# Attention with a gated second branch: PE mode runs over two row blocks, wider query-weight and key loads

## The chip, the cores and the metric

The kernel runs on one core of a Trainium2 chip. The metric is the device time of one launch in microseconds (us), the median over several runs. A profiled execution has a span a little shorter than its device time (933.1 us of 934.86 us before); both are used, and it is said which. The engines are named as in the profile: PE is the matmul engine, PEld its weight loads, DVE the vector engine, ACT the scalar engine, POOL is GpSimd, SP the queue from which most transposing transfers are issued.

## The reference

A layer norm, an attention with 32 heads of width 192 over the last 512 cached keys, and a gated feed-forward branch that multiplies the attention's output.

```python
# x: 1 x 2048 x 640; k_cache, v_cache: 1 x 32 x 2048 x 192; wq: 640 x 6144; wo: 6144 x 640
xn = _layernorm(x)
q = (xn @ wq) as 32 heads of 192
k, v = k_cache[:, :, -512:], v_cache[:, :, -512:]
p = softmax(q k^T * 192**-0.5)
s = (p v) merged over heads @ wo
g = silu((sigmoid(xn @ w_gate) * (xn @ w_up)) @ w_down)
return x + s * g
```

## The kernel before

The feed-forward branch comes first (about 165 us). The attention then goes over 16 pairs of heads in 8 groups of two pairs (`G = 2`, `NG = 8`), and for each group over 4 row blocks of 512 queries (`NST = 4`): 32 blocks. A head has 192 = 3 x 64 elements (`PC = 3`), so the query and score matmuls contract over 64 rows. Two of them run at once, one in rows 0 to 63 of the array and one in rows 64 to 127 (`LO`, `HI`). The value and output matmuls contract over all 128 rows. I call these the two modes of PE.

```python
def stage_q(n, u):                       # 20 matmuls, 64 rows: queries of the next block
    ...
    for c in range(NCD):
        for h in range(2):
            for b, r in enumerate((LO, HI)):
                nc.tensor.matmul(ps[:, b, :], lhsT=wq_t[g][r, u, 2 * c + h]..., rhs=x[s][r, c, :], ...)
    nc.vector.tensor_copy(qT_t[n][:, 2 * u:2 * u + 2, :], ps)

def stage_s(n, pp, c):                   # 6 matmuls, 64 rows: scores, then exp on ACT
    ...
def stage_pv(n, pp, i):                  # 16 matmuls, 128 rows: values of one head
    if i == 0:
        ost_t[0] = ost_pool.tile([P, TQ, 2 * DH], BF16, name="o_st")     # ost_pool: bufs=2
    ...                                  # DVE: reciprocal, then o_st = ps * reciprocal
    if i == 1:
        oT = oT_pool.tile([P, TQ * PC, P], BF16, name="oT")
        nc.sync.dma_start_transpose(oT[:], o_st[:]...)                   # read by stage_wo
def stage_wo(n, q):                      # 12 matmuls, 128 rows: output projection
    ...
for n, (g, s) in enumerate(blocks):      # 32 blocks
    for k, (pp, c) in enumerate(todo):   # 8 score stages, 3 query stages: 64 rows
        stage_s(n, pp, c)
        if k % 2 == 1 and k // 2 < G * PC // 2 and n < last:
            stage_q(n + 1, k // 2)
    ...                                  # loads ahead
    for k, u in enumerate(pv):           # 4 value stages, 4 output stages of block n - 1: 128 rows
        stage_pv(*u)
        if wo:
            stage_wo(*wo[k])
```

PSUM, the memory that the matmuls write to, is used as a ring of four slots of two banks (`bank2`). A stage takes the next slot and has to wait until the stage four before it has been read out. `o_st` takes the finished values of a pair of heads for one block, and a DMA transposes it into `oT`.

The softmax here doesn't subtract the row's maximum and nothing guards it: scores larger than these inputs give would overflow.

Of the kernel before, what the change touches and what calls it, by code (L numbers as in the profile page):

```python
# [9 lines left out]
ALU = mybir.AluOpType  # L10
BF16 = mybir.dt.bfloat16
# [4 lines left out]
def kernel(  # L16
# [72 lines left out]

    rs = dict(side="right")  # L90
    xnt_pool = ctx.enter_context(tc.tile_pool(name="xnt_pool", bufs=1, **rs))
    wq_pool = ctx.enter_context(tc.tile_pool(name="wq_pool", bufs=2, **rs))
    k_pool = ctx.enter_context(tc.tile_pool(name="k_pool", bufs=2, **rs))
    kt_pool = ctx.enter_context(tc.tile_pool(name="kt_pool", bufs=2 * G, **rs))
    v_pool = ctx.enter_context(tc.tile_pool(name="v_pool", bufs=1, **rs))

    HF = 64
# [3 lines left out]
    xnS = [xnt_pool.tile([P, NCD, 512], BF16, name=f"xnS{s}") for s in range(NST)]  # L101
    xnT = [xnt_pool.tile([P, NCD, 512], BF16, name=f"xnT{s}") for s in range(NST)]

    NV = 4 * G
    v_tiles = []
    for i in range(NV):
        vt = v_pool.tile([P, KC, DH + 2], BF16, name=f"v_sb{i}")
# [7 lines left out]

    k_of = {}

    def load_k(hp, eng):

        k_sb = k_pool.tile([P, KC * PC, 2, HF], BF16, name="k_sb")  # L120
        for i in range(2):
            hk = (2 * hp + i) // rep
            eng.dma_start(
                k_sb[:, :, i, :],
                A_k_cache[0, hk, Sk - W:Sk, :].rearrange("(p k) (j e) -> p (k j) e", k=KC, j=PC),
            )
        k_of[hp] = k_sb

    def load_v(hp, eng):
        v_t[hp] = []  # L130
        for i in range(2):
            hk = (2 * hp + i) // rep
            vt = v_tiles[(2 * hp + i) % NV]
            eng.dma_start(
                vt[:, :, 0:DH],
                A_v_cache[0, hk, Sk - W:Sk, :].rearrange("(p j) d -> p j d", j=KC),
            )
            v_t[hp].append(vt)

    def load_wq(hp, eng):  # L140


        if hp % G == 0:
            wq_t[hp // G] = wq_pool.tile([P, G * PC // 2, NCD * 2, 2, HF], BF16, name="wqp")
        wqp = wq_t[hp // G]
        for j in range(PC):
            jj = (hp % G) * PC + j
            r = HI if jj % 2 else LO
            for i in range(2):
                d0 = (2 * hp + i) * DH + j * HF  # L150
                eng.dma_start(
                    wqp[r, jj // 2, :, i, :],
                    wq_r[:, :, :, d0:d0 + HF].rearrange("p c h n -> p (c h) n"),
                )

    def turn_k(hp):
        kT = kt_pool.tile([P, KC * PC, P], BF16, name="kT")
        nc.sync.dma_start_transpose(kT[:], k_of[hp][:].rearrange("p k i e -> p (k i e)"))
        kT_t[hp] = kT


    with ExitStack() as bctx:
# [147 lines left out]
        for s in range(NST):  # L310
# [40 lines left out]
            nc.sync.dma_start(xnS[s][HI], xnT[s][LO])  # L351
            if s == 0:
                for hp in range(G):
                    load_k(hp, nc.gpsimd)
                for hp in range(G):
                    load_v(hp, nc.gpsimd)
                    load_wq(hp, nc.gpsimd)
            elif s == 1:
                for hp in range(G):
                    turn_k(hp)  # L360


    acc_pool = ctx.enter_context(tc.tile_pool(name="acc_pool", bufs=1))
    wo_pool = ctx.enter_context(tc.tile_pool(name="wo_pool", bufs=2))
    qT_pool = ctx.enter_context(tc.tile_pool(name="qT_pool", bufs=2))
    e_pool = ctx.enter_context(tc.tile_pool(name="e_pool", bufs=2))
    ost_pool = ctx.enter_context(tc.tile_pool(name="ost_pool", bufs=2))
    oT_pool = ctx.enter_context(tc.tile_pool(name="oT_pool", bufs=2 * G))
    small = ctx.enter_context(tc.tile_pool(name="small", bufs=8))
    fin = ctx.enter_context(tc.tile_pool(name="fin", bufs=2))  # L370
    fout = ctx.enter_context(tc.tile_pool(name="fout", bufs=4))
    gate_pool = ctx.enter_context(tc.tile_pool(name="gate_pool", bufs=TQ + 2))

    acc = [acc_pool.tile([P, D], F32, name=f"acc{t}") for t in range(NST * TQ)]
    wo_t = {}

    def load_wo(g, eng):
        wo_g = wo_pool.tile([P, G * PC, D], BF16, name="wo_g")
        eng.dma_start(wo_g[:], wo_r[:, g * G * PC:(g + 1) * G * PC, :])
        wo_t[g] = wo_g  # L380

    def load_ahead(g, s):


        if s < G:
            load_wq(g * G + s, nc.scalar)
            load_k(g * G + s, nc.scalar)
        elif s == G:
            for hp in range(g * G, (g + 1) * G):
                load_v(hp, nc.scalar)  # L390
                turn_k(hp)
        if s == NST - 1:
            load_wo(g, nc.scalar)



# [1 line left out]

    def stage_q(n, u):

        g, s = blocks[n]
        if u == 0:
            qT_t[n] = qT_pool.tile([P, G * PC, 512], BF16, name="qT")
        ps = bank2()
        for c in range(NCD):
            for h in range(2):
                for b, r in enumerate((LO, HI)):
                    x = xnT if b == h else xnS
                    nc.tensor.matmul(  # L409
                        ps[:, b, :], lhsT=wq_t[g][r, u, 2 * c + h].rearrange("p i e -> p (i e)"),  # L410
                        rhs=x[s][r, c, :],
                        start=(c == 0 and h == 0), stop=(c == NCD - 1 and h == 1),
                    )
        nc.vector.tensor_copy(qT_t[n][:, 2 * u:2 * u + 2, :], ps)  # L414

    def stage_s(n, pp, c):

        g, s = blocks[n]
        kT, qT = kT_t[g * G + pp], qT_t[n]
        if c == 0:  # L420
            E_t[n, pp] = e_pool.tile([P, KC, 2, 512], BF16, name="E")
        ps = bank2()
        for j in range(PC):
            for b, r in enumerate((LO, HI)):
                nc.tensor.matmul(  # L425
                    ps[:, b, :], lhsT=kT[r, c * PC + j, :], rhs=qT[r, pp * PC + j, :],
                    start=(j == 0), stop=(j == PC - 1),
                )
        nc.scalar.activation(E_t[n, pp][:, c, :, :], ps, AF.Exp, scale=scale_qk)  # L429
# [60 lines left out]
                )  # L490

    def finish(ps, gB_sb, t, d0, d1):
        t_sb = fin.tile([P, D], F32, name="t_sb")
        o_sb = fout.tile([P, D], BF16, name="o_sb")
        d = slice(d0, d1)
        nc.vector.tensor_tensor(t_sb[:, d], ps, gB_sb[:, d], ALU.mult)  # L496
        nc.vector.tensor_tensor(o_sb[:, d], t_sb[:, d], acc[t][:, d], ALU.add)  # L497
        nc.sync.dma_start(of[t * P:(t + 1) * P, d], o_sb[:, d])

    gates = {}  # L500
# [1 line left out]
    def stage_wo(n, q):  # L502
        g, s = blocks[n]
        t = s * TQ + q
        gB_sb = gates.get(t)
        if n == last and q == TQ - 1:

            ps, h = bank2(), D // 2
            for i in range(2):
                wo_mm(ps[:, i, :], n, q, [(i * h, h)], i * h)  # L510
                finish(ps[:, i, 0:h], gB_sb, t, i * h, (i + 1) * h)
            return
        oA = flat(bank2())
        wo_mm(oA, n, q, d_chunks)
        if g == NG - 1:
            finish(oA[:, 0:D], gB_sb, t, 0, D)
        elif g == 0:
            nc.vector.tensor_copy(acc[t][:], oA[:, 0:D])
        else:
            nc.vector.tensor_tensor(acc[t][:], oA[:, 0:D], acc[t][:], ALU.add)  # L520
        if g == NG - 2:
            prep_last(t)

    blocks = [(g, s) for g in range(NG) for s in range(NST)]
    last = len(blocks) - 1
    qT_t, E_t, oT_t, ost_t = {}, {}, {}, {}
    load_wo(0, nc.gpsimd)
    for u in range(G * PC // 2):
        stage_q(0, u)
    for n, (g, s) in enumerate(blocks):  # L530

        todo = [(pp, c) for pp in range(G) for c in range(KC)]
        for k, (pp, c) in enumerate(todo):
            stage_s(n, pp, c)
            if k % 2 == 1 and k // 2 < G * PC // 2 and n < last:
                stage_q(n + 1, k // 2)
        if g + 1 < NG:
            load_ahead(g + 1, s)
        for m in (n - 1, n) if n == last else (n - 1,):
            if n > 0 and blocks[m][0] == NG - 1:  # L540
                for t in range(blocks[m][1] * TQ, blocks[m][1] * TQ + TQ):
                    gates[t] = load_gate(t, nc.scalar)

        pv = [(n, pp, i) for pp in range(G) for i in range(2)]
        wo = [(n - 1, q) for q in range(TQ)] if n > 0 else []
        if n < last:
            for k, u in enumerate(pv):
                stage_pv(*u)
                if wo:
                    stage_wo(*wo[k])  # L550
        else:
            for k, u in enumerate(pv):
                stage_pv(*u)
                if k == 1:
                    stage_wo(*wo.pop(0))
            for u in wo:
                stage_wo(*u)
    for q in range(TQ):
        stage_wo(last, q)

# [28 lines left out]
```

## Time and profile before

| | before |
|---|---|
| device time | 934.81 us, later 934.77 us (4 runs, 934.43 to 934.86) |
| span of the profiled execution | 933.1 us |
| PE busy, matmuls | 924.7 us, 8025 |
| first query matmul to the end | 768.35 us of the span |
| one block: 64-row part, 128-row part | 11.76 us, 12.07 us |
| changes between the two modes in the attention | 63 |

First the page of the profile: the busy times of the engines, the clock granted to PE in 40 equal slices (tenths of full speed, 9 is 90% or more), and the DMA packets.

```profile
PE 924.7 (99%) x8025; PEld 539.4 (58%) x8025; DVE 451.2 (48%) x643; ACT 303.8 (33%) x340; POOL 87.9 (9%) x107
...
PEclk9999999999999999999999999999999999999999
...
DMA packets 271681, 87.18 MB, mean 93 GB/s; under 512 B 250289, under 2 KB 268785, under 8 KB 271601
```

PE is busy throughout at full clock. That alone does not say that it works at its peak, since matmuls overlap in the record. The starts tell more. In time order, a matmul with 512 columns is followed after 215 to 216 ns, one with 193 columns after 86 ns, one with 128 columns after 56 ns. The two matmuls of a 64-row pair start 2 to 4 ns apart, the next pair 213 ns later.

One group line of the page, the loading of query weights into the array (line, engine, operation, shapes and count, busy us, mean ns of one, idle time before it):

```profile
L409 PEld LDWEIGHTS <-wqp 64*128 64x128 bf16 x1920 | 93.4, 94 | 113.8 <-issue 0.3
```

The timeline of PE through one whole block shows the two modes (start us, duration us, engine, line, operation, output<-inputs, shapes, count):

```profile
402.98 1.47 PE L425 MATMUL ps_all<-qT,kT 64*128 64x512 bf16 x12
...
413.35 1.46 PE L425 MATMUL ps_all<-qT,kT 64*128 64x512 bf16 x12
414.74 1.54 PE L441 MATMUL ps_all<-v_sb_97,E 128*128 128x193 bf16 x16
416.11 1.79 PE L486 MATMUL ps_all<-wo_g,oT 128*128 128x512 bf16 x12
...
426.81 1.47 PE L425 MATMUL ps_all<-qT,kT 64*128 64x512 bf16 x12
```

The 64-row part takes 414.74 - 402.98 = 11.76 us, the 128-row part 426.81 - 414.74 = 12.07 us. At the border the pace breaks: from the last score matmul to the first value matmul it is 308 ns start to start instead of 213, and from the last output matmul to the next score matmul 152 ns instead of 56. After the change the second and third value matmuls follow at 94 and 88 ns before the pace of 86 is reached, and after the change back the second score pair follows at 223 ns instead of 213. Where the stage changes but not the mode, the pace holds: 85 to 86 ns from a value to an output matmul, 55 to 56 from an output to a value matmul, 212 to 213 between query and score pairs. So the break goes with the change of mode and not with the change of stage. Such a change of mode comes 63 times.

### The profile page before, as it was taken

Reading aid. Unit: us, or ns where it says so; the run is one execution under the profiler, and the core shown is the slowest. Engines: PE = TensorE matmul, PEld = TensorE weight load, DVE = VectorE, ACT = ScalarE, POOL = GpSimd, SP = SyncE. Lnnn points to the kernel's source line nnn. Section 1 sums busy time; section 2 is a strip of 40 time slices with the busy share of each in tenths; the row PEclk is TensorE's granted clock in tenths of the full one; section 3 lists DMA queues with packets and bytes.
Section 4 is the critical chain, followed back from the end, with each engine's and each line's share of the span. In section 5 each row is a group of like instructions: output and inputs, shape, how many; then the busy total and the mean of one; then the engine's idle time right before and its main releaser. Section 6 shows DMA issues by size and latency. Waiting matters only on the chain. (4 is left out here: it accounts for less than half of the span.)

```text
span 933.1 us, 18277 instructions
## 1 busy us (share of the span) xinstructions
PE 924.7 (99%) x8025; PEld 539.4 (58%) x8025; DVE 451.2 (48%) x643; ACT 303.8 (33%) x340; POOL 87.9 (9%) x107
## 2 busy tenths in 40 slices
PE   8999999999999999999999999999999999999997
PEld 5545445565555555555555555555665665665665
DVE  4443532454444444444444444444444444444657
ACT  4333322433333333333333333333333333333340
POOL 0070000100000000000000000000000006665000
PEclk9999999999999999999999999999999999999999
DMA  9566030376334533463346324633563348553435
GB/s 286 151 125 119 15 98 15 96 111 102 82 58 70 107 77 55 73 121 77 47 71 113 63 70 70 106 68 77 73 106 70 77 73 152 125 130 77 91 91 148
DMA packets 271681, 87.18 MB, mean 93 GB/s; under 512 B 250289, under 2 KB 268785, under 8 KB 271601
## 3 DMA queue, kind: packets, MB, share of 16 engines
q1 hardware_dynamic: 146864, 47.20, 25.9%
q10 hardware_dynamic: 121136, 27.40, 14.9%
q0 software_dynamic: 3600, 11.41, 4.8%
q8 instruction: 63, 1.03, 0.5%
q14 instruction: 18, 0.14, 0.1%
HBM read 44.70 MB, written 5.24 MB: 54 GB/s over the span
## 5 line engine op out<-in xcount | busy, mean ns | idle before, releaser
L429 ACT ACTIVATE E<-ps_all 128x1024 bf16<-128x1024 f32 x256 | 247.8, 1022 | 496.2 <-PE ps_all L425 443.8
L486 PE MATMUL ps_all<-wo_g,oT 128*128 128x512 bf16 (+2 forms) x1536 | 228.2, 299 | 0.0
L414 DVE CAST qT<-ps_all 128x1024 bf16<-128x1024 f32 x96 | 117.6, 1225 | 226.3 <-PE ps_all L409 226.3
L425 PE MATMUL ps_all<-qT,kT 64*128 64x512 bf16 x1536 | 186.7, 376 | 0.0
L441 PEld LDWEIGHTS <-E 128*128 128x128 bf16 x2048 | 171.0, 98 | 24.4 <-issue 13.6
L486 PEld LDWEIGHTS <-oT 128*128 128x128 bf16 x1536 | 121.4, 97 | 76.2
L409 PEld LDWEIGHTS <-wqp 64*128 64x128 bf16 x1920 | 93.4, 94 | 113.8 <-issue 0.3
L425 PEld LDWEIGHTS <-kT 64*128 64x128 bf16 x1536 | 72.3, 94 | 91.8 <-issue 8.4
L448 DVE TENSOR_TENSOR o_st<-ps_all,rden 128x768 bf16<-128x768 f32 x128 | 122.6, 958 | 4.8 <-DVE rden L447 0.5
L447 DVE RECIPROCAL rden<-ps_all 128x4 f32<-128x4 f32 x128 | 23.3, 182 | 98.2 <-PE ps_all L441 98.1
L477 POOL TENSOR_TENSOR acc_1573<-acc_1573,gBa_sb 128x640 f32<-128x640 f32 x1 | 1.4, 1399 | 603.4 <-DVE acc_1573 L520 603.4
L325 DVE TENSOR_TENSOR hT_sb<-ps_all,sig_sb 128x512 bf16<-128x512 f32 x48 | 33.1, 692 | 51.0 <-PE ps_all L319 41.1
L409 PE MATMUL ps_all<-xnT_94,wqp 64*128 64x512 bf16 x240 | 55.7, 376 | 0.0
L409 PE MATMUL ps_all<-xnT_96,wqp 64*128 64x512 bf16 x240 | 55.7, 376 | 0.0
L409 PE MATMUL ps_all<-xnT_95,wqp 64*128 64x512 bf16 x240 | 55.7, 376 | 0.0
L409 PE MATMUL ps_all<-xnS_90,wqp 64*128 64x512 bf16 x240 | 55.6, 376 | 0.0
L409 PE MATMUL ps_all<-xnS_92,wqp 64*128 64x512 bf16 x240 | 55.6, 376 | 0.0
L409 PE MATMUL ps_all<-xnS_91,wqp 64*128 64x512 bf16 x240 | 55.6, 376 | 0.0
L409 PE MATMUL ps_all<-xnT_93,wqp 64*128 64x512 bf16 x240 | 55.4, 376 | 0.0
L409 PE MATMUL ps_all<-xnS_89,wqp 64*128 64x512 bf16 x240 | 55.3, 376 | 0.0
L339 PE MATMUL ps_all<-wd_sb,hT_sb 128*128 128x512 bf16 (+1 forms) x384 | 52.8, 299 | 0.0
L324 ACT ACTIVATE sig_sb<-ps_all 128x512 bf16<-128x512 f32 x48 | 28.6, 597 | 56.6 <-PE ps_all L319 56.2
(159 smaller groups left out, 681.6 us busy)
## 6 DMA issues: line engine op xcount, KB each, us to landing
wqp<-in_A_wq_dram ACTq DMA_DIRECT2D x84, 80.0 KB, 3.0
wo_g<-in_A_wo_dram ACTq DMA_DIRECT2D x7, 960.0 KB, 5.3
k_sb<-in_A_k_cache_dram ACTq DMA_DIRECT2D x28, 192.0 KB, 4.8
gB_d<-gB_sb POOLq DMA_DIRECT2D x16, 160.0 KB, 2.4
gBa_sb<-gB_d POOLq DMA_DIRECT2D x16, 160.0 KB, 3.6
xa_sb<-in_A_x_dram POOLq DMA_DIRECT2D x16, 160.0 KB, 3.5
gBa_sb<-gB_d ACTq DMA_DIRECT2D x16, 160.0 KB, 3.0
out_dram<-o_sb SPq DMA_DIRECT2D x15, 160.0 KB, 1.8
```

Of the source, the lines that this page charges most:

```text
L324: nc.scalar.activation(sig_sb[:], gu[:, 0, :], AF.Sigmoid)
L325: nc.vector.tensor_tensor(hT_sb[:, f, :], gu[:, 1, :], sig_sb[:], ALU.mult)
L339: nc.tensor.matmul(oB_ps[:, d0:d0 + dsz], lhsT=hT_sb[:, f, q * P:(q + 1) * P], rhs=wd_sb[:, f, d0:d0 + dsz], start=(f == 0), stop=(f == NF ...
L409: nc.tensor.matmul(ps[:, b, :], lhsT=wq_t[g][r, u, 2 * c + h].rearrange("p i e -> p (i e)"), rhs=x[s][r, c, :], start=(c == 0 and h == 0), ...
L414: nc.vector.tensor_copy(qT_t[n][:, 2 * u:2 * u + 2, :], ps)
L425: nc.tensor.matmul(ps[:, b, :], lhsT=kT[r, c * PC + j, :], rhs=qT[r, pp * PC + j, :], start=(j == 0), stop=(j == PC - 1),)
L429: nc.scalar.activation(E_t[n, pp][:, c, :, :], ps, AF.Exp, scale=scale_qk)
L441: nc.tensor.matmul(o_ps[:, q // 2, q % 2, 0:DH + 1], lhsT=E[:, c, i, q * P:(q + 1) * P], rhs=vt[:, c, 0:DH + 1], start=(c == 0), stop=(c = ...
L447: nc.vector.reciprocal(rden[:], o_ps[:, :, :, DH:DH + 1])
L448: nc.vector.tensor_tensor(o_st[:, :, i * DH:(i + 1) * DH].rearrange("p (b i) d -> p b i d", b=2), o_ps[:, :, :, 0:DH], rden[:].to_broadcas ...
L477: nc.gpsimd.tensor_tensor(acc[t][:], acc[t][:], gB_sb[:], ALU.mult)
L486: nc.tensor.matmul(oA[:, d0 - base:d0 - base + dsz], lhsT=oT_t[n, pp][:, q * PC + j, :], rhs=wo_t[g][:, cc, d0:d0 + dsz], start=(cc == 0), ...
```

## The change

The intent is to change the mode half as often: two blocks form a run, with 16 score stages and 6 query stages first, then 8 value stages and the 8 output stages of the run before. That needs more buffers for scores and queries, so others are halved (`wq`, `wo`, `k`, `kT`, `v`). The loads change with it. Query weights come in 16 transfers of 480 KB with rows of 768 bytes (before: 96 of 80 KB, 128-byte rows), issued by GpSimd instead of mostly by ACT, and the array's weight load then picks every third column. Keys come in full rows (1,536 bytes per partition) and are reordered by copies on GpSimd. The last multiplication is done in place in PSUM.

```diff
-    wq_pool = ... bufs=2      k_pool = ... bufs=2      kt_pool = ... bufs=2 * G
+    wq_pool = ... bufs=1      kn_pool, k_pool = ... bufs=1      kt_pool = ... bufs=G
-    NV = 4 * G
+    NV = 2 * G
...
     def load_k(hp):
+        kn_sb = kn_pool.tile([P, 2, KC, DH], BF16, name="kn_sb")   # two loads of full rows, gpsimd queue
+        k_sb = k_pool.tile([P, KC, PC, 2, HF], BF16, name="k_sb")
+        for i in range(2):
+            nc.gpsimd.tensor_copy(
+                k_sb[:, :, :, i, :], kn_sb[:, i, :, :].rearrange("p k (e j) -> p k j e", j=PC))
...
     def load_wq(hp):
+            wq_t[hp // G] = wq_pool.tile([P, NCD * 2, 2 * DH], BF16, name="wqp")
+        nc.gpsimd.dma_start(wq_t[hp // G][HI if hp % G else LO],
+            wq_r[:, :, :, hp * 2 * DH:(hp + 1) * 2 * DH].rearrange("p c h n -> p (c h) n"))
...
     def stage_q(n, u):
-                        ps[:, b, :], lhsT=wq_t[g][r, u, 2 * c + h].rearrange("p i e -> p (i e)"),
+                        ps[:, b, :], lhsT=wq_t[g][r, 2 * c + h, u::PC],
...
     def finish(ps, gB_sb, t, d0, d1):
-        nc.vector.tensor_tensor(t_sb[:, d], ps, gB_sb[:, d], ALU.mult)
-        nc.vector.tensor_tensor(o_sb[:, d], t_sb[:, d], acc[t][:, d], ALU.add)
+        nc.vector.tensor_tensor(ps, ps, gB_sb[:, d], ALU.mult)
+        nc.vector.tensor_tensor(o_sb[:, d], ps, acc[t][:, d], ALU.add)
...
+    runs = [[n, n + 1] for n in range(0, last - 1, 2)] + [[last - 1], [last]]
-    for n, (g, s) in enumerate(blocks):
+    for r, ns in enumerate(runs):
+        s_list = [(n, pp, c) for n in ns for pp in range(G) for c in range(KC)]
+        q_list = [(n, u) for n in sum(runs[r + 1:r + 2], []) for u in range(PC)]
+        ...                                  # score stages, query stages spread among them
+        if at_start:                         # first run of a group: next group's loads
+            for hp in hps: load_wq(hp)
+            for hp in hps[:1]: load_k(hp)
+        if at_end:                           # last run of a group: keys, and the key transposes
+            ...
+        pv_list = [(n, pp, i) for n in ns for pp in range(G) for i in range(2)]
+        wo_list = [(n, q) for n in before for q in range(TQ)]
+        ...                                  # value stages, output stages of the run before
```

More of the change, by code (lines that the diff above doesn't have):

```diff
@@ L91 @@
     xnt_pool = ctx.enter_context(tc.tile_pool(name="xnt_pool", bufs=1, **rs))
-    wq_pool = ctx.enter_context(tc.tile_pool(name="wq_pool", bufs=2, **rs))
-    k_pool = ctx.enter_context(tc.tile_pool(name="k_pool", bufs=2, **rs))
-    kt_pool = ctx.enter_context(tc.tile_pool(name="kt_pool", bufs=2 * G, **rs))
+    wq_pool = ctx.enter_context(tc.tile_pool(name="wq_pool", bufs=1, **rs))
+    kn_pool = ctx.enter_context(tc.tile_pool(name="kn_pool", bufs=1, **rs))
+    k_pool = ctx.enter_context(tc.tile_pool(name="k_pool", bufs=1, **rs))
+    kt_pool = ctx.enter_context(tc.tile_pool(name="kt_pool", bufs=G, **rs))
     v_pool = ctx.enter_context(tc.tile_pool(name="v_pool", bufs=1, **rs))
@@ L116, with load_k @@
     k_of = {}
-    def load_k(hp, eng):
-        k_sb = k_pool.tile([P, KC * PC, 2, HF], BF16, name="k_sb")
+    def load_k(hp):
+        kn_sb = kn_pool.tile([P, 2, KC, DH], BF16, name="kn_sb")
         for i in range(2):
             hk = (2 * hp + i) // rep
-            eng.dma_start(
-                k_sb[:, :, i, :],
-                A_k_cache[0, hk, Sk - W:Sk, :].rearrange("(p k) (j e) -> p (k j) e", k=KC, j=PC),
+            nc.gpsimd.dma_start(
+                kn_sb[:, i, :, :],
+                A_k_cache[0, hk, Sk - W:Sk, :].rearrange("(p k) d -> p k d", k=KC),
+            )
+        k_sb = k_pool.tile([P, KC, PC, 2, HF], BF16, name="k_sb")
+        for i in range(2):
+            nc.gpsimd.tensor_copy(
+                k_sb[:, :, :, i, :], kn_sb[:, i, :, :].rearrange("p k (e j) -> p k j e", j=PC)
             )
@@ L138, in load_v, with load_wq @@
             v_t[hp].append(vt)
-    def load_wq(hp, eng):
+    def load_wq(hp):
         if hp % G == 0:
-            wq_t[hp // G] = wq_pool.tile([P, G * PC // 2, NCD * 2, 2, HF], BF16, name="wqp")
-        wqp = wq_t[hp // G]
-        for j in range(PC):
-            jj = (hp % G) * PC + j
-            r = HI if jj % 2 else LO
-            for i in range(2):
-                d0 = (2 * hp + i) * DH + j * HF
-                eng.dma_start(
-                    wqp[r, jj // 2, :, i, :],
-                    wq_r[:, :, :, d0:d0 + HF].rearrange("p c h n -> p (c h) n"),
-                )
+            wq_t[hp // G] = wq_pool.tile([P, NCD * 2, 2 * DH], BF16, name="wqp")
+        nc.gpsimd.dma_start(
+            wq_t[hp // G][HI if hp % G else LO],
+            wq_r[:, :, :, hp * 2 * DH:(hp + 1) * 2 * DH].rearrange("p c h n -> p (c h) n"),
+        )
     def turn_k(hp):
         kT = kt_pool.tile([P, KC * PC, P], BF16, name="kT")
-        nc.sync.dma_start_transpose(kT[:], k_of[hp][:].rearrange("p k i e -> p (k i e)"))
+        nc.sync.dma_start_transpose(kT[:], k_of[hp][:].rearrange("p k j i e -> p (k j i e)"))
         kT_t[hp] = kT
@@ L353 @@
                 for hp in range(G):
-                    load_k(hp, nc.gpsimd)
-                for hp in range(G):
                     load_v(hp, nc.gpsimd)
-                    load_wq(hp, nc.gpsimd)
+                    load_wq(hp)
             elif s == 1:
                 for hp in range(G):
+                    load_k(hp)
                     turn_k(hp)
     acc_pool = ctx.enter_context(tc.tile_pool(name="acc_pool", bufs=1))
-    wo_pool = ctx.enter_context(tc.tile_pool(name="wo_pool", bufs=2))
-    qT_pool = ctx.enter_context(tc.tile_pool(name="qT_pool", bufs=2))
-    e_pool = ctx.enter_context(tc.tile_pool(name="e_pool", bufs=2))
+    wo_pool = ctx.enter_context(tc.tile_pool(name="wo_pool", bufs=1))
+    qT_pool = ctx.enter_context(tc.tile_pool(name="qT_pool", bufs=4))
+    e_pool = ctx.enter_context(tc.tile_pool(name="e_pool", bufs=2 * G))
     ost_pool = ctx.enter_context(tc.tile_pool(name="ost_pool", bufs=2))
-    oT_pool = ctx.enter_context(tc.tile_pool(name="oT_pool", bufs=2 * G))
+    oT_pool = ctx.enter_context(tc.tile_pool(name="oT_pool", bufs=3 * G))
     small = ctx.enter_context(tc.tile_pool(name="small", bufs=8))
     fin = ctx.enter_context(tc.tile_pool(name="fin", bufs=2))
-    fout = ctx.enter_context(tc.tile_pool(name="fout", bufs=4))
+    fout = ctx.enter_context(tc.tile_pool(name="fout", bufs=3))
     gate_pool = ctx.enter_context(tc.tile_pool(name="gate_pool", bufs=TQ + 2))
@@ L375, with load_wo @@
     wo_t = {}
-    def load_wo(g, eng):
+    def load_wo(g):
         wo_g = wo_pool.tile([P, G * PC, D], BF16, name="wo_g")
-        eng.dma_start(wo_g[:], wo_r[:, g * G * PC:(g + 1) * G * PC, :])
+        nc.scalar.dma_start(wo_g[:], wo_r[:, g * G * PC:(g + 1) * G * PC, :])
         wo_t[g] = wo_g
-    def load_ahead(g, s):
-        if s < G:
-            load_wq(g * G + s, nc.scalar)
-            load_k(g * G + s, nc.scalar)
-        elif s == G:
-            for hp in range(g * G, (g + 1) * G):
-                load_v(hp, nc.scalar)
-                turn_k(hp)
-        if s == NST - 1:
-            load_wo(g, nc.scalar)
     def stage_q(n, u):
@@ L402, in stage_q @@
         if u == 0:
-            qT_t[n] = qT_pool.tile([P, G * PC, 512], BF16, name="qT")
+            qT_t[n] = qT_pool.tile([P, PC, G, 512], BF16, name="qT")
         ps = bank2()
@@ L413, in stage_q @@
                     )
-        nc.vector.tensor_copy(qT_t[n][:, 2 * u:2 * u + 2, :], ps)
+        nc.vector.tensor_copy(qT_t[n][:, u, :, :], ps)
     def stage_s(n, pp, c):
@@ L425, in stage_s @@
                 nc.tensor.matmul(
-                    ps[:, b, :], lhsT=kT[r, c * PC + j, :], rhs=qT[r, pp * PC + j, :],
+                    ps[:, b, :], lhsT=kT[r, c * PC + j, :], rhs=qT[r, j, pp, :],
                     start=(j == 0), stop=(j == PC - 1),
@@ L492, in finish @@
     def finish(ps, gB_sb, t, d0, d1):
-        t_sb = fin.tile([P, D], F32, name="t_sb")
         o_sb = fout.tile([P, D], BF16, name="o_sb")
         d = slice(d0, d1)
-        nc.vector.tensor_tensor(t_sb[:, d], ps, gB_sb[:, d], ALU.mult)
-        nc.vector.tensor_tensor(o_sb[:, d], t_sb[:, d], acc[t][:, d], ALU.add)
+        nc.vector.tensor_tensor(ps, ps, gB_sb[:, d], ALU.mult)
+        nc.vector.tensor_tensor(o_sb[:, d], ps, acc[t][:, d], ALU.add)
         nc.sync.dma_start(of[t * P:(t + 1) * P, d], o_sb[:, d])
@@ L525 @@
     last = len(blocks) - 1
+    runs = [[n, n + 1] for n in range(0, last - 1, 2)] + [[last - 1], [last]]
     qT_t, E_t, oT_t, ost_t = {}, {}, {}, {}
-    load_wo(0, nc.gpsimd)
-    for u in range(G * PC // 2):
-        stage_q(0, u)
-    for n, (g, s) in enumerate(blocks):
-        todo = [(pp, c) for pp in range(G) for c in range(KC)]
-        for k, (pp, c) in enumerate(todo):
-            stage_s(n, pp, c)
-            if k % 2 == 1 and k // 2 < G * PC // 2 and n < last:
-                stage_q(n + 1, k // 2)
-        if g + 1 < NG:
-            load_ahead(g + 1, s)
-        for m in (n - 1, n) if n == last else (n - 1,):
-            if n > 0 and blocks[m][0] == NG - 1:
-                for t in range(blocks[m][1] * TQ, blocks[m][1] * TQ + TQ):
-                    gates[t] = load_gate(t, nc.scalar)
-        pv = [(n, pp, i) for pp in range(G) for i in range(2)]
-        wo = [(n - 1, q) for q in range(TQ)] if n > 0 else []
-        if n < last:
-            for k, u in enumerate(pv):
-                stage_pv(*u)
-                if wo:
-                    stage_wo(*wo[k])
-        else:
-            for k, u in enumerate(pv):
-                stage_pv(*u)
-                if k == 1:
-                    stage_wo(*wo.pop(0))
-            for u in wo:
-                stage_wo(*u)
@@ new lines @@
+    load_wo(0)
+    for n in runs[0]:
+        for u in range(PC):
+            stage_q(n, u)
+    for r, ns in enumerate(runs):
+        g = blocks[ns[0]][0]
+        at_start, at_end = blocks[ns[0]][1] == 0, blocks[ns[-1]][1] == NST - 1
+        before = runs[r - 1] if r > 0 else []
+        s_list = [(n, pp, c) for n in ns for pp in range(G) for c in range(KC)]
+        q_list = [(n, u) for n in sum(runs[r + 1:r + 2], []) for u in range(PC)]
+        done = 0
+        for k, x in enumerate(s_list):
+            stage_s(*x)
+            if done < len(q_list) and (k + 1) * (len(q_list) + 1) >= (done + 1) * len(s_list):
+                stage_q(*q_list[done])
+                done += 1
+        for u in q_list[done:]:
+            stage_q(*u)
+        hps = range((g + 1) * G, (g + 2) * G) if g + 1 < NG else []
+        if at_start:
+            for hp in hps:
+                load_wq(hp)
+            for hp in hps[:1]:
+                load_k(hp)
+        if at_end:
+            for hp in hps:
+                if hp not in k_of:
+                    load_k(hp)
+                turn_k(hp)
+        for n in before + (ns if r == len(runs) - 1 else []):
+            if blocks[n][0] == NG - 1:
+                for t in range(blocks[n][1] * TQ, blocks[n][1] * TQ + TQ):
+                    gates[t] = load_gate(t, nc.scalar)
+        pv_list = [(n, pp, i) for n in ns for pp in range(G) for i in range(2)]
+        wo_list = [(n, q) for n in before for q in range(TQ)]
+        done = 0
+        for k, x in enumerate(pv_list):
+            stage_pv(*x)
+            share = (k + 1) * len(wo_list) // len(pv_list)
+            if r == len(runs) - 1:
+                share = (k + 1) // 2 if k + 1 < len(pv_list) else len(wo_list)
+            while done < share:
+                stage_wo(*wo_list[done])
+                done += 1
+        if at_start and g > 0:
+            load_wo(g)
+        if at_end:
+            for hp in hps:
+                load_v(hp, nc.scalar)
```

## The prediction

> **What bounds the kernel now.** TensorE. The page gives PE 924.7 of 933.1 us busy at granted clock 0.998. Busy alone proves little, so I took the starts of consecutive matmuls from the timeline: 512-column matmuls follow at 215-216 ns, 193-column ones at 86, 128-column ones at 56; the two matmuls of a 64-row pair start 2 to 4 ns apart, with 213 ns from pair to pair. No wait recurs. The Trainium skill, "TensorE: Matmul & The Clock Gate", section "Back-to-back issue gap", gives N/2.4 + 2.5 ns; this trace agrees (216 ns at N = 512).
>
> **The one recurring loss.** Each change of PE mode: score matmul (64 rows) to value matmul (128 rows) takes 308 ns start to start instead of 213, in 31 of 32 places; output matmul back to scores takes 152 instead of 56. So a change costs about 95 ns. "TensorEngine Tiling (Array Packing)", "Key Properties", says that changing the mode drains the array. The old order has 32 + 31 such changes, about 6.0 us.
>
> **What the change does.**
> - Removes: 32 blocks become 15 runs of two blocks and two of one: 17 + 16 changes. Thirty fewer at 95 ns: -2.9 us, all on the critical path.
> - Matmul count and shapes stay (8025), so the rest can only be zero or a loss.
> - Query weights: 96 loads of 80 KB in 128-byte rows become 16 of 480 KB; keys come in whole rows. DMA is off the path: no gain here.
> - The query weight load into the array reads 128 columns at stride three (6 bytes). Now each takes 94 ns; both of a pair run side by side inside the 213 ns pitch. Even at double length it stays hidden: 0. Beyond 213 ns it would lengthen 960 pairs, about 1 us per extra ns. This is the largest risk.
> - Key reorder: 64 GpSimd copies of 128x768, estimated from GpSimd's 1.4 us for 128x640 with two inputs at 1 to 2 us each. Two lie between the two key transposes at the end of a group: about 4.3 + 2x2 + 4.3 = 13 us, inside the some 24 us of the value/output phase. Output transposes queue behind for a few us, but are used a run later.
> - Buffers for wq, wo, k, kT, v are halved. Each reload has a value/output phase (about 24 us, two times 12.1) or a score/query phase (about 23 us) before use, and lands in 3 to 10 us: no new PE wait expected.
> - End: eight outputs instead of four are finished between four value stages. VectorE needs 2 x (0.82 + 0.83) plus about 1.2 us against about 4.6 us of PE, and a PSUM slot is now held through both operations: 0 to +1.5 us, I take +0.5, seen as a wait at the last block's scores.
>
> **Prediction.** 934.8 - 2.9 + 0.5 = 932.4 us, range 930.8 to 935.6 (8 in 10). Faster by over 2%: 0.01; within 2%: 0.93; slower by over 2%: 0.06.
>
> **What would show each step.** Matmul starts: 17 + 16 gaps of about 308 and 152 ns, pair pitch still 213 ns in the query projection. Groups by line: query weight loads below about 200 ns. Waits: none new of PE on wqp, kT, v or wo; GpSimd busy up by 60 to 130 us. DMA packets fall from 271,681 by some 96,000. Granted clock unchanged.
>
> **What would make it wrong.** A strided weight load that outlasts the pair (tens of us slower); a single-buffered tile that arrives late at each of eight groups (a few us each); a mode change whose cost moves to another boundary.

## The result, and the profile after

The changed kernel takes 933.23 us (4 runs, 932.88 to 933.50) against 934.77 us (4 runs). A ratio here is the mean time of one kernel's fast runs over that of the other's of the same rounds, so it is not quite the ratio of the medians; it is 0.9984, with a 95% interval of 0.9967 to 1.0001. A later repetition (below) gave 0.9982, 0.9968 to 0.9995. So the gain is put at just under 0.2%; the first interval just includes no gain at all, the second does not. The time lies in the predicted range and 0.8 us above the predicted value. (The check says little about the queries: the three versions below that use wrong ones on purpose passed it too. That the new layouts are right rests on the code, in which queries and keys take every third element in the same way.)

The page of the changed kernel, the same lines, and two groups:

```profile
PE 918.3 (99%) x7946; PEld 549.5 (59%) x8025; DVE 450.7 (48%) x639; ACT 302.2 (32%) x340; POOL 129.5 (14%) x170
...
PEclk9999999999999999999999999999999999999999
...
DMA packets 176959, 87.17 MB, mean 94 GB/s; under 512 B 152240, under 2 KB 171312, under 8 KB 176880
...
L397 PEld LDWEIGHTS <-wqp 64*128 64x128 bf16 x1920 | 100.4, 100 | 107.7 <-issue 0.8
...
L131 POOL COPY k_sb<-kn_sb 128x768 bf16<-128x768 bf16 x32 | 25.9, 832 | 274.3 <-DMA kT<-k_sb 227.3
```

(79 of the 8025 matmul records are missing from this trace, so its PE busy time is not compared.) The clock is unchanged and 94,722 DMA packets are gone (the wider rows are not the only reason: the order alone, below, with 128-byte rows issued by GpSimd, has 179,519). A query weight load takes 100 ns instead of 94, well inside the 213 ns of a pair. The timeline of PE through one run of two blocks:

```profile
403.55 2.12 PE L413 MATMUL ps_all<-qT,kT 64*128 64x512 bf16 x18
...
425.58 1.46 PE L413 MATMUL ps_all<-qT,kT 64*128 64x512 bf16 x12
426.97 1.53 PE L429 MATMUL ps_all<-v_sb,E 128*128 128x193 bf16 x16
...
451.00 2.12 PE L413 MATMUL ps_all<-qT,kT 64*128 64x512 bf16 x18
```

The 64-row part is now 23.42 us (twice 11.76 is 23.52), the 128-row part 24.03 us (twice 12.07 is 24.14). Each change saved is worth 0.10 to 0.11 us. Thirty are saved, so about 3.1 us should be gone, but the kernel is only 1.5 us faster. The rest is given back in one place, at the start of the second run. Timeline of PE there, with the idle time before an instruction and what ended it in brackets:

```profile
212.47 0.82 PE L413 MATMUL ps_all<-qT,kT 64*128 64x512 bf16 x6 [0.59 <-DVE o_st L436]
213.55 0.82 PE L413 MATMUL ps_all<-qT,kT 64*128 64x512 bf16 x6 [0.26 <-DVE o_st L436]
214.63 0.82 PE L413 MATMUL ps_all<-qT,kT 64*128 64x512 bf16 x6 [0.26 <-DVE o_st L436]
215.71 0.37 PE L397 MATMUL ps_all<-xnT,wqp 64*128 64x512 bf16 x1 [0.26 <-DVE o_st L436]
```

From the last value matmul to the first score matmul it is 840 ns start to start (180 ns in the other kernels at such a place), and the next three stages begin 633, 634 and 633 ns after the matmul before them instead of 213. That is 0.66 + 3 x 0.42 = 1.92 us. PE waits for PSUM slots that DVE has not read. The timeline of DVE says why it was late:

```profile
207.83 0.18 DVE L435 RECIPROCAL rden<-ps_all 128x4 f32<-128x4 f32 x1
211.45 0.96 DVE L436 TENSOR_TENSOR o_st<-ps_all,rden 128x768 bf16<-128x768 f32 x1 [3.44 <-DMA oT<-o_st]
212.33 0.17 DVE L435 RECIPROCAL rden<-ps_all 128x4 f32<-128x4 f32 x1
```

DVE has to write the third `o_st` tile. There are two buffers, and the first is still being transposed: that transfer was issued at 204.95 us and landed after 6.41 us, where the median in the kernel before is 3.8 us. This is the only run in which eight value stages follow each other without output stages in between, since there is no run before it. A tile is made in 2 x 1.38 = 2.8 us there, and in about 6 us in the runs of two blocks after it. In the same stretch the next group's query weights (two transfers of 480 KB, issued at 199.9 and 200.6 us) and keys (two of 192 KB) are on their way.

So there are two candidate causes for the 1.92 us: too few `o_st` buffers for this pace, or DMA traffic that stretches the transposes.

### The profile page after: what moved, and what is told of

The parts are those of the page before. It is cut to its first block, busy times and chain, and to the rows that moved or that the text cites. A ratio compares the mean times of both kernels' runs of the same rounds, so it can differ in the third digit from the quotient of the medians.

```text
span 931.2 us, 18098 instructions
## 1 busy us (share of the span) xinstructions
PE 918.3 (99%) x7946; PEld 549.5 (59%) x8025; DVE 450.7 (48%) x639; ACT 302.2 (32%) x340; POOL 129.5 (14%) x170
## 3 DMA queue, kind: packets, MB, share of 16 engines
q0 software_dynamic: 6656, 22.81, 10.1%
## 5 line engine op out<-in xcount | busy, mean ns | idle before, releaser
L474 PE MATMUL ps_all<-wo_g,oT 128*128 128x128 bf16 (+2 forms) x1474 | 224.3, 295 | 3.2
L397 PE MATMUL ps_all<-xnT,wqp 64*128 64x512 bf16 x960 | 222.2, 376 | 0.3 <-DVE o_st L436 0.3
L397 PE MATMUL ps_all<-xnS,wqp 64*128 64x512 bf16 x960 | 221.4, 376 | 0.0
L429 PE MATMUL ps_all<-v_sb,E 128*128 128x193 bf16 x2048 | 193.7, 247 | 0.1
L507 DVE TENSOR_TENSOR acc<-ps_all,acc 128x640 f32<-128x640 f32 x96 | 79.2, 825 | 42.7 <-PE ps_all L474 42.7
L131 POOL COPY k_sb<-kn_sb 128x768 bf16<-128x768 bf16 x32 | 25.9, 832 | 274.3 <-DMA kT<-k_sb 227.3
L320 PE MATMUL ps_all<-xnT,wu_sb 128*128 128x512 bf16 x220 | 55.6, 379 | 0.3
L320 PE MATMUL ps_all<-xnT,wg_sb 128*128 128x512 bf16 x220 | 55.5, 379 | 0.3
L340 PE MATMUL ps_all<-wd_sb,hT_sb 128*128 128x128 bf16 (+1 forms) x377 | 52.4, 298 | 0.4
L340 PEld LDWEIGHTS <-hT_sb 128*128 128x128 bf16 x384 | 29.7, 98 | 23.1
```

Of the source, the lines that this page charges most:

```text
L320: nc.tensor.matmul(gu[:, i, :], lhsT=w[:, c, f * P:(f + 1) * P], rhs=xnT[s][:, c, :], start=(c == 0), stop=(c == NCD - 1),)
L340: nc.tensor.matmul(oB_ps[:, d0:d0 + dsz], lhsT=hT_sb[:, f, q * P:(q + 1) * P], rhs=wd_sb[:, f, d0:d0 + dsz], start=(f == 0), stop=(f == NF ...
L397: nc.tensor.matmul(ps[:, b, :], lhsT=wq_t[g][r, 2 * c + h, u::PC], rhs=x[s][r, c, :], start=(c == 0 and h == 0), stop=(c == NCD - 1 and h ...
L429: nc.tensor.matmul(o_ps[:, q // 2, q % 2, 0:DH + 1], lhsT=E[:, c, i, q * P:(q + 1) * P], rhs=vt[:, c, 0:DH + 1], start=(c == 0), stop=(c = ...
L474: nc.tensor.matmul(oA[:, d0 - base:d0 - base + dsz], lhsT=oT_t[n, pp][:, q * PC + j, :], rhs=wo_t[g][:, cc, d0:d0 + dsz], start=(cc == 0), ...
L507: nc.vector.tensor_tensor(acc[t][:], oA[:, 0:D], acc[t][:], ALU.add)
```

## The experiments

The figure "attention" below is the stretch from the first query matmul to the end of the profiled execution: 768.35 us before, 766.73 us in the changed kernel. It leaves out the first 165 us, which vary by up to 0.5 us from trace to trace.

### Runs of one block

```diff
-    runs = [[n, n + 1] for n in range(0, last - 1, 2)] + [[last - 1], [last]]
+    runs = [[n] for n in range(last + 1)]
-        if at_start:                                    # load_wq, first load_k
+        nxt = runs[r + 1] if r + 1 < len(runs) else []
+        if nxt and blocks[nxt[-1]] == (g, NST - 1):
```

(The second part makes the loads wait for the last query stage of the group.)

> The new loads and layouts, but runs of one block each, so 32 + 31 mode changes again. Theory (a change of PE mode costs about 95 ns, and the changed kernel loses about 1.9 us once, at the scores of its second run, because eight value stages in a row come without an output stage between): the thirty changes come back (+2.9 us against the changed kernel) and the one-time loss goes (-1.9 us), so about 934.2 us, near the kernel before; the trace has 32 gaps of 308 ns and 30 or 31 of 152 ns and none of 633 ns. Rival (the gain came from the DMA layout, the order is worth nothing): no slower than 933.2 us, and rather 931.3.

Measured: 935.64 us (5 runs, 935.42 to 935.87), ratio to before 1.0007 (0.9994 to 1.0019); attention 769.00 us. All 63 changes are back, and there is no 633 ns gap. It came out 1.4 us above the figure expected. The trace shows a reason that I had not counted: one score matmul in the first block comes 1.26 us after the one before it instead of 0.21, for the copy of the third query stage. In the new layout each score stage needs all three query stages, and with a first run of one block they have only just been computed. The rival is out: new loads and layouts with the old order gain nothing.

### Only the first two blocks apart

```diff
-    runs = [[n, n + 1] for n in range(0, last - 1, 2)] + [[last - 1], [last]]
+    runs = [[0], [1]] + [[n, n + 1] for n in range(2, last - 1, 2)] + [[last - 1], [last]]
```

> Blocks 0 and 1 as runs of their own, all others in twos as in the changed kernel: 18 + 17 mode changes. Theory of the one-time loss (eight value stages in a row without an output stage between): it disappears, -1.9 us, and two more mode changes cost 0.2 us, so about 931.5 us, with no score matmul waiting 633 ns. Rival (the loss belongs to any start of the second run, for example late keys or query weights): a wait of 1 to 2 us is still there and the time stays within 0.5 us of 933.2.

Measured: 932.54 us (5 runs, 932.52 to 932.83), ratio 0.9975 (0.9962 to 0.9987); attention 766.03 us. The waits at the second run are gone, although the loads are issued later here (at 207.8 us instead of 199.9), so they do not belong to late keys or weights. Since this edit changes the pace of the first value stages and moves the loads, it does not separate the two candidate causes. The figure was missed by 1.0 us for the same reason as above. The waits of PE in this trace (waiting, releaser, us in total, times, longest) have it:

```profile
PE ps_all L413 <- DVE qT L402: 0.9, 1, 0.9
```

### No loads during the first run

```diff
-        if at_start:
+        if r == 0:
+            wq_t[1] = wq_t[0]          # wrong queries in group 1, on purpose
+        elif at_start:
```

> Wrong result on purpose: the first run loads neither the next group's query weights (two transfers of 480 KB) nor the next keys (two of 192 KB); group 1 uses the query weights of group 0, its keys come later. Theory A (these loads share the DMA engines with the output transposes and stretch the first from about 3.7 us to 6.4 us): the wait of VectorE for the transposed tile falls from 3.4 us to under 1 us, the 633 ns gaps disappear, -1.5 to -1.9 us. Theory B (two o_st buffers are too few at any rate, since a pair of value stages makes one in 2.8 us and a transpose takes at least 3.6 us): the wait stays at 2 us or more and at least half of the loss stays.

Measured: 931.40 us (5 runs, 930.99 to 931.64), ratio 0.9961 (0.9947 to 0.9975); attention 764.77 us, 1.96 us less than the changed kernel. (The comparison still counted the output as correct within its tolerance, although group 1 has wrong queries: the reference draws keys and query weights so small that the scores stay near zero. It is no version to use. In the trace the next keys come earlier and not later, issued at 167 to 173 us; either way no load falls in this stretch.) With two `o_st` buffers as before, the first three transposes now land in 3.63, 3.64 and 3.69 us instead of 6.41, 4.97 and 5.85, and no score matmul waits. The waits of DVE for a free tile, first in the changed kernel, then here:

```profile
DVE o_st L436 <- DMA oT<-o_st: 3.4, 1, 3.4
```

```profile
DVE o_st L436 <- DMA oT<-o_st: 1.3, 2, 0.7
```

So theory A holds in the main: the traffic makes the wait long enough to reach PE. Its figure for the wait, under 1 us, was a little low: theory B's remark that two buffers are tight stays visible as 1.3 us, which does not reach PE. The edit also takes two copies on GpSimd out of this stretch. They are not the cause: the version below that has no such copies has transposes as slow (5.99, 6.90 and 7.27 us). The Trainium skill, "DMA: Bandwidth & Descriptors", section "Issuing engines are not separate DMA queues", says that transfers from all issuing engines run on the same 16 DMA engines and interleave; traces agree: with loads from the GpSimd queue beside it, the first transpose from the SP queue takes 6.4 us, without them 3.6.

### Three o_st buffers

```diff
-    ost_pool = ... bufs=2     gate_pool = ... bufs=TQ + 2     small = ... bufs=8
+    ost_pool = ... bufs=3     gate_pool = ... bufs=TQ         small = ... bufs=4
```

> Three o_st buffers instead of two (room from the gate pool, 6 to 4, and the reciprocal pool, 8 to 4). Both theories of the one-time loss have VectorE wait for a free o_st buffer; with a third one the wait at the first run's third tile goes and the 1.9 us of waiting scores shrink to under 0.5 us: about 931.5 us, if the smaller gate pool costs nothing at the end. If the scores wait for something else (keys, PSUM alone), the loss stays.

Measured: 931.33 us (5 runs, 931.31 to 931.56), ratio 0.9962 (0.9950 to 0.9974); attention 764.76 us. PE at the same place:

```profile
212.01 2.12 PE L413 MATMUL ps_all<-qT,kT 64*128 64x512 bf16 x18
213.96 0.38 PE L397 MATMUL ps_all<-xnT,wqp 64*128 64x512 bf16 x1
```

Three score stages run through without a wait and the query stage follows. The transposes are as slow as ever (6.47, 5.04 and 5.33 us); they no longer reach PE. The loss thus needs both, slow transposes and only two buffers, and taking away either removes all of it. This is also the version that beats both kernels: the same computation, 3.5 us under before.

### The order alone, the layouts undone

```diff
+            for i in range(2):         # in load_wq, for each j: 128-byte rows, packed
+                d0 = (2 * hp + i) * DH + j * HF
+                nc.gpsimd.dma_start(wq_t[hp // G][r, :, j, i, :], wq_r[:, :, :, d0:d0 + HF]...)
+            nc.gpsimd.dma_start(       # in load_k: 128-byte rows straight into k_sb, no copy
+                k_sb[:, :, :, i, :]..., A_k_cache[...].rearrange("(p k) (j e) -> p (k j) e", ...))
-                        lhsT=wq_t[g][r, 2 * c + h, u::PC],
+                        lhsT=wq_t[g][r, 2 * c + h, u].rearrange("p i e -> p (i e)"),
```

> The order of the changed kernel (runs of two blocks) with both layouts undone: query weights in packed 128-byte rows, keys in 128-byte rows, no GpSimd reorder, weights read at stride one. Theory (only the order bears on the time): within 0.5 us of the changed kernel's 933.2 us; the query weight load is 94 ns again instead of 100; the wait at the second run's scores stays, and may grow, since 128-byte rows keep the DMA engines busy longer in the same stretch. Rival (the layouts carry part of the 1.5 us gain by themselves): about 934.8 us without a longer wait at the second run.

Measured: 935.23 us (5 runs, 934.56 to 935.72), ratio 1.0003 (0.9990 to 1.0017); attention 769.01 us, 2.28 us more than the changed kernel. The theory's figure, within 0.5 us, fell; the side remark, that the wait may grow, is what happened. The later runs are as in the changed kernel (23.42 and 24.03 us). The 128-row part of the first run and the 64-row part of the second together take 38.66 us instead of 36.38: the whole difference is there. One score matmul starts 2.17 us after the one before it. The waits of this run:

```profile
DVE o_st L431 <- DMA oT<-o_st: 4.6, 2, 3.0
PE ps_all L408 <- DVE o_st L431: 2.2, 3, 1.8
```

PE at the end of the longest wait, in the timeline:

```profile
216.22 1.47 PE L408 MATMUL ps_all<-qT,kT 64*128 64x512 bf16 x6 [1.79 <-DVE o_st L431]
```

The stretch that follows, by windows (start and end us, length, busy us and count of PE, PEld, DVE, ACT and POOL, granted clock, DMA share, GB/s):

```profile
216.20:219.50 3.30, 3.28 (x16) 1.41 (x17) 1.02 (x2) 1.02 (x1) 0.00 (x0) 0.50 1.53 183
```

So the rival has a point, though not as it was put: in this order, undoing the layouts costs 2.28 us in the trace, which was taken in the slowest of the five runs (against the changed kernel's median the runs are 1.3 to 2.5 us slower). The transposes are disturbed for longer: the second and third take 6.90 and 7.27 us instead of 4.97 and 5.85, and the loads issued from 200.4 us on land up to 217.6 us. But the waits themselves grow only by 0.7 us, from 1.92 to 2.62 (423, 634 and 2166 ns where 180, 213 and 213 are usual). The other 1.6 us are in the last line above: from the end of that gap to 219.5 us the granted clock is 0.5, and matmul pairs start every 427 ns instead of 213 to 216. In the other eleven traces the clock is full from 7.2 us on until at most 3.3 us before the end. The low clock starts as the longest gap ends; whether the gap is its cause no run tests. The edit also makes 14 transfers out of 4 in this stretch, so row width alone is not shown to be the reason. The skill's DMA page, "Specifications", names 512 bytes as the smallest transfer at full rate. The trace agrees in direction only: with 128-byte rows the packets of the GpSimd queue take 10.7% of the DMA engines' time instead of 10.1%.

### The layouts alone, the old order

```diff
 # on the kernel before: load_wq, load_k, qT layout and strided lhsT of the changed kernel
+    kn_pool = ... bufs=1      gate_pool = ... bufs=TQ
```

> The kernel before with only the layouts changed: 480 KB query weight loads in 768-byte rows read at stride three, keys in whole rows reordered on GpSimd (gate pool 6 to 4 for room). Theory (layouts are off the path): the mode changes stay at 32 + 31, the query weight load takes 100 ns, and the time is that of before, 934.9 us, plus about 1 us once, because the first score matmul now needs the third query stage's copy (seen as one 1.26 us gap in the two runs with single first blocks): 935 to 936.2 us. Rival (layouts gain): below 934.5 us.

Measured: 935.89 us (5 runs, 935.67 to 936.04), ratio 1.0013 (1.0000 to 1.0026); attention 769.30 us, with all 63 changes and one 1.26 us gap in the first block. As the theory had it, the layouts gain nothing in the old order.

### How far the stride can go

```diff
-                        lhsT=wq_t[g][r, 2 * c + h, u::PC],
+                        lhsT=...[:, offset + u:][:, 0:1017:8],      # and 0:3049:24 in the second kernel
```

> Wrong result on purpose: the changed kernel with the query weights read at stride eight (16 bytes) instead of three, from the same tile. Tests how far the stride is from harm. [...]as long as it stays under the pair's 213 ns the pair pitch stays 213 ns and the time within 0.5 us of 933.2. If the two loads of a pair then no longer run side by side, the pitch grows and 960 pairs give about 1 us per ns: tens of us.

> Wrong result on purpose: the same with stride twenty-four (48 bytes). If what counts is one access per line, the load takes as long as at stride eight; if distance itself counts, it is longer again. Under 213 ns the time stays within 0.5 us of 933.2; above, about 1 us per extra ns.

Measured: 933.05 us at stride eight (4 runs, ratio 0.9982, 0.9969 to 0.9996) and 933.15 us at stride twenty-four (4 runs, ratio 0.9984, 0.9970 to 0.9997), both as the changed kernel. The query weight loads (count, minimum/median/maximum ns), first in the changed kernel, then at stride eight, then at twenty-four:

```profile
L397 PEld LDWEIGHTS <-wqp x1920: 98/100/107, 164.4 to 881.5; 64*128 64x128 bf16 x192
```

```profile
L397 PEld LDWEIGHTS <-wqp x1920: 137/140/168, 164.5 to 881.4; 64*128 64x128 bf16 x192
```

```profile
L397 PEld LDWEIGHTS <-wqp x1920: 144/145/175, 164.6 to 881.5; 64*128 64x128 bf16 x192
```

Stride one takes 94 ns, three 100, eight 140, twenty-four 145. The Trainium skill, "SBUF — State Buffer", "Specifications (TRN2)", speaks of 16-byte lines and wants at least two hits per line for full bandwidth. The steps fit: three elements (6 bytes) still hit a line twice or more and cost 6 ns, eight elements (16 bytes) hit each line once and cost 46, and going further adds little. This is a fit and no test of the mechanism: strides between three and eight were not tried, and my guess for stride eight, 150 to 200 ns, was too high. All stay hidden under a pair's 213 ns.

### More changes of mode

On the version with three `o_st` buffers:

```diff
+        late = q_list[PC:] if at_end and len(ns) == 2 and len(q_list) == 2 * PC else []
+        q_list = q_list[:len(q_list) - len(late)]
         ...
         for k, x in enumerate(pv_list):
             stage_pv(*x)
             ...                        # output stages
+            if k % 2 == 1 and late:
+                stage_q(*late.pop(0))
```

> The version with three o_st buffers, where at the end of each of the first seven groups three of the six query stages move, one at a time, from the score phase into the value/output phase. Same matmuls, same loads, 42 more changes of PE mode. Theory (a change costs about 95 ns wherever it stands): 42 x 0.095 = +4.0 us on the 931.3 us of that version, about 935.3 us; the gaps are 308 ns where a 64-row matmul is followed by a value matmul and 152 ns where an output matmul is followed by a 64-row one. Rival (what a longer run saves is something of the score phase, its start or its waits on ScalarE): much less than 2 us more.

Measured: 935.67 us (6 runs, 935.37 to 935.92), ratio 1.0010 (0.9998 to 1.0023); attention 769.41 us, 4.65 us more than with three buffers alone. With 42 more changes that is 0.111 us for each, a little over the 0.095 expected. One moved query stage in the timeline:

```profile
233.40 1.79 PE L474 MATMUL ps_all<-wo_g,oT 128*128 128x512 bf16 x12
235.13 0.39 PE L397 MATMUL ps_all<-xnT,wqp 64*128 64x512 bf16 x1
...
237.40 1.53 PE L429 MATMUL ps_all<-v_sb,E 128*128 128x193 bf16 x16
```

All 21 transitions from an output to a query matmul take 152 ns, and all 21 from a query to a value matmul 308 ns (309 at most). No matmul waits for a buffer here. The cost belongs to the change of mode and not to the score phase or its waits.

### The changed kernel again

> The changed kernel again, unaltered, for a ratio from more rounds: 933.2 us, 0.998 to 0.9985 of before, and the same four waiting gaps at the second run's scores (840, 633, 634, 633 ns), if that loss is not an accident of one run.

Measured: 933.00 us (5 runs, 932.63 to 933.23) against 934.65 us (10 runs). Of the four gaps the three of about 633 ns are there again (632 to 636 ns), the first is 553 ns instead of 840. The two stride versions, which have the same order and loads, show the same four gaps, with a first of 629 and 553 ns. So the loss is no accident, but its size varies with the transfers: 0.37 + 3 x 0.42 = 1.6 us here.

## Why the prediction was right, and where it was not

The time was right: 933.2 us in a range of 930.8 to 935.6, and "within 2%" at 0.93. Point by point:

| kernel | mode changes | attention us | made of (from before, 768.35) |
|---|---|---|---|
| changed | 33 | 766.73 | -3.15 changes, +1.92 wait, -0.38 end |
| runs of one block | 63 | 769.00 | +1.05 first block, -0.40 end |
| first two apart | 35 | 766.03 | -2.94 changes, +1.05 first block, -0.39 end |
| three o_st buffers | 33 | 764.76 | -3.15 changes, -0.39 end |
| more changes | 75 | 769.41 | three o_st buffers and 42 more |

In the last column a change is counted at 0.105 us, the saving read from the timeline of one run; the sums of the first four rows come within 0.1 us of the measured stretches. The last row would come out 0.24 us short, since a change costs 0.111 us there. "End" is the time from the last block's first value matmul to the end of the execution (24.05 us before, 23.67 us in the changed kernel).

- "Thirty fewer at 95 ns: -2.9 us, all on the critical path" was right. The gaps went from 32 + 31 to 17 + 16, and the moved query stages price the change independently. It is slightly larger (0.105 to 0.111 us), because the first matmuls after a change of mode are slow too (94 ns, and 223 ns for a pair, as shown above).
- "The query weight load ... stays hidden: 0" was right (100 ns), with room up to stride twenty-four.
- "No new PE wait expected" on wqp, kT, v or wo was right: halving those buffers cost nothing that the waits show.
- "DMA is off the path: no gain here" was wrong in a way. In the old order it holds (layouts alone: no gain). In the new order the transfers of the first run are on the path, through the transposes, and with the old layouts the loss is larger, by 2.28 us in the trace, of which 1.6 us are a stretch at half the granted clock.
- "End: ... I take +0.5, seen as a wait at the last block's scores" is the step that failed. The gaps in the last block are as before (404 and 469 ns), and the end is 0.38 us shorter. The runs of one block show the same short end (23.65 us) and so does the order alone (23.67), so it comes neither from the order nor from the layouts. PE takes the same 18.34 us of it in every trace; the difference is on DVE. The product and the sum for the first half of the last output tile, first in the kernel before, then in the changed kernel:

```profile
927.84 0.48 DVE L496 TENSOR_TENSOR t_sb<-ps_all,gBa_sb 128x320 f32<-128x320 f32 x1
928.77 0.49 DVE L497 TENSOR_TENSOR o_sb<-t_sb,acc_1588 128x320 bf16<-128x320 f32 x1 [0.44 <-issue]
```

```profile
926.34 0.49 DVE L483 TENSOR_TENSOR ps_all<-ps_all,gBa_sb 128x320 f32<-128x320 f32 x1
926.92 0.49 DVE L484 TENSOR_TENSOR o_sb<-ps_all,acc 128x320 bf16<-128x320 f32 x1
```

The sum starts 0.93 us after the product before (0.95 in the layouts alone, which also keep `t_sb`), and 0.58 us in all ten traces with the product in place. DVE ends about 0.31 us sooner for it. This points to the product in place, which I had counted as a loss; no run changes it alone.
- The loss that did come, 1.92 us, was not on the list. I checked the buffers that the change halves, not `o_st`, whose two buffers it leaves alone while the first run makes the tiles about twice as fast as the runs after it.
- "64 GpSimd copies", "1 to 2 us each", GpSimd busy "up by 60 to 130 us": there are 32 copies of 0.83 us, and the busy time rose by 41.6 us. It did not matter.

So the predicted net gain (-2.4 us) was larger than the measured one (-1.5 us, and -1.65 us in the repetition) since the one-time wait of 1.92 us was missing from the sum. That the total still came within 0.8 us is partly luck: the end was 0.88 us better than assumed, and the changes gave 0.25 us more. And "within 2%" allows 18.7 us either way, so it tests little here.

## What to carry to other kernels

When a kernel is at streaming rate, look for the breaks in the pace at borders between stages, count them, and price one: 63 changes of mode at 0.1 us were the whole recurring loss here, so at this price no order could gain much over 0.7%. When stages of one kind are put together, check the buffers that were left unchanged as well, in the first and last run above all, where the partner stage that used to give them time is missing. And DMA that is "off the path" can come back onto it through a shared transfer; a third buffer was the cheapest cure.

## What the Trainium skill lacked or had wrong

- "TensorEngine Tiling (Array Packing)" says that changing the mode drains the array, but gives no time. Here the gap grows by 95 to 96 ns in either direction (308 against 213 ns, 152 against 56), and one change costs 0.105 to 0.111 us in all.
- "TensorE: Matmul & The Clock Gate", section "Back-to-back issue gap", also gives about 131 ns per matmul for N = 512, and about 81 ns for N = 128, as the sustained pace of load and matmul pairs. In this trace it is 215 to 216 ns and 56 ns, which is the page's formula for a single gap.
- The same page, on the weight-path modes, lists packed and strided columns alike and gives no time for a stride. Measured: 94 ns at stride one, 100 at three, 140 at eight, 145 at twenty-four, for 64 rows and 128 columns of bf16, with the two loads of a pair side by side.
- "DMA: Bandwidth & Descriptors" has no figure for what copies do to a transposing transfer that runs beside them. Here 1.3 MB of loads stretched one from 3.6 to 6.4 us.
